# Two layers of attention on one core: the same steps with another table of order, engines and buffers

## The chip, the cores and the metric

The kernel runs on one core of a Trainium2 chip. The metric is the device time of one execution in microseconds. Five engines work beside each other in the core, each through its own queue of instructions in order: TensorE (PE in the profile), VectorE (DVE), ScalarE (ACT), GpSimd (POOL), and SyncE (SP), which here only issues DMA. An engine that waits for a semaphore holds up everything queued behind the waiting instruction.

## The reference

```python
# 1: two-way cross attention of x (8,8,512,64) and state (8,8,32,64), scale 1/8
a     = softmax(scale * x @ state.T);      xread = a @ state
a2    = softmax(scale * state @ x.T);      sread = a2 @ x
y     = concat([xread, sread], axis=2)     # -> (8, 544, 512): 512 x tokens, 32 state tokens
# 2: mixture of 4 attention experts, 2 of them per token, causal
topk, w = two largest of y @ w_gate, softmax over the two
for e in range(4):
    q, k, v = y @ wq[e], y @ wk[e], y @ wv[e]                 # 512 -> 64
    ye  = softmax(causal(scale * q @ k.T)) @ v @ wo[e]        # 64 -> 512
    out += w_e * ye                                           # for tokens that chose e
```

## The kernel before

The eight batches run through the same stages, and several batches are in work at a time. Nearly all matrix products are three products of fp16 halves: a value is kept as a high part and a low part (the rest), and high x high, high x low and low x high are added in a PSUM bank (`PROD`). So nearly every tensor passes through a pair of steps that make the high part (mostly a copy on ACT) and the low part (a subtraction on DVE or POOL).

Per batch, `front` loads and splits x (`xn` to `xh`), turns it by a DMA transpose or by TensorE (`xT`), forms the softmax over the state tokens (scores in a bank, maximum `mb`, exponentials `eb`, sum and reciprocal `sbm`, product `eb` x `sbm`, turned and split into `at`), multiplies the state with the weights (`gs`), and from `at` and `gs` makes values (`v`), keys (`kt`), gate logits (`lg`, weights `wgt`) and queries: a query tile is read out of its bank times a 0/1 mask of the token's experts (`qf` <- bank, `m`; the mask is `m6` in the code), split into `qh` and turned by DMA into `qm`. `probs` computes a query tile's scores for the chosen experts (bank <- `kt`, `qm`), adds the causal mask, takes the maximum (`mx`), the exponential, splits it (`ph`) and has it turned by DMA (`pt`). `reads` multiplies `pt` with `v`, normalises (`su`, `c`, `z`), splits (`zh`, or `zhp` for two tiles at once) and turns; `result` multiplies with `wo` and stores (`o`). The state tokens of two batches are handled together by `side` and `tail`: in `tail`, L1078 makes flags of which experts each of 128 rows has chosen (`m4`, 128 x 4, from `twg`), and the matmul behind it spreads them over a bank (bank <- `identh`, `m`). The trace leaves numbers out of names, so `m4`, `m6` and the maxima of the scores are all `m` there.

None of this sets the order. The calls only record steps: `st.step` keeps an instruction or a group of them with what it reads and writes, 1867 in all. A step that more than one engine could do is recorded with several ways by `small`, `tiny`, `pair`, `split`, `low`, `out_of_bank` and `st.either` (L209): ACT, DVE or POOL for a high part, POOL or DVE for a low part, ACT or DVE for the copy of a bank, and so on. A recorded step has the buffer it belongs to, and a buffer kind has several slots.

`run` (L255) then unpacks three compressed tables from the constant `ORDER`: the order in which the 1867 steps are issued, the way that each takes, and the slot that each buffer gets. It issues every step in that order on line 265, so nearly all instructions of the trace are of L265; they are told apart by the names of their tiles. What stands in the tables was worked out beforehand, and so was `FILL` (L19): a list with one entry for each dummy matmul (`band` 128 x 128 with 128 x 512 zeros into a bank "warm", read by nobody, L511 to L514), whose place in the queue is again in the table. The program holds no other scheduler: each engine runs its instructions in the order issued, and semaphores keep the dependencies.

Of the kernel before, what the change touches and what calls it, by code (L numbers as in the profile page):

```python
# [18 lines left out]
CFG = dict(FILL=(1.0, 1.4, 1.8, 2.2, 2.6, 3.0, 3.4, 3.8, 4.2, 4.6, 5.0,), RA=-1, RG=1, RV=2, RK=2, ZL=3, GP=1, PT=4, ZM=4, SM=4, QM=4, SIDE=32, FB=1, PX=1, PA=2, LB=1, xn=4, W0=-33, PACE=37.0, MU=2, XP=(1,), QP=(0,), LAG=2,  # L19
           FRONT=1.5, FSPAN=1.0, TSPAN=1.3, TOFF=1.2, KT=3, p32=3, ph=2, at=1, et=1, gs=1, xh=4, a2=1, o=4, sn=1, qf=2,  # L20
           n_eb=1, n_e2=1, n_a2t=1, n_xt_tail=2, n_z32=3, n_z=2, n_zh=2, n_tq=1, n_tv=2, n_tpt=1, n_tz=1, n_pt=3, D1=6, DA=6)
ORDER = (
    (
        "c-jrsgJKYB7y!`E|CZKJE!P@qORFurZM9|Fwr$(CZQHhO+xETZB~AhGf-H~^d>}CdKyHW+QIHkFAR%OiypRYALk0+ef{+!90RRF4gMdORh=A"
        "0P4c9;#NC2xK1`K>*E%-wcaF7E0AT1<^valLb!U`w@)u9CB#AQ$eGQkPRjiC^M<scbEVo4|uh4B<5g_>{@Vxa;Q!J?Q8D?%-(1o`na1VUvv1"
        "KFVpTmWx44+o$&cz`FwgQ}1ROTk%a0CnIT)P-u07cW9XD2Dam5~PDhPzYK>F31A~ur$<%Ah-+#aXG}n73cta;VNu_?AR6Z;WcOronR{z!f<Q"
# [2 lines left out]
        "y`-^_17^TNh)<Pp7R-ckkbq`GeH;&oX%WQYF}M$L=uN9}F)V>K_y&Ba6gI$z;7d#45j=*qcn=;xWvqdB;0e5ir|=d0s0u!Vcklw<LrqLb&*3"
        "<HgjM_!>R>}`jHU4de1}?C6<<Lk{03#P2_~X-SR2b?HEfEX;0IL4pU@gV!$<0X>+w6iqh{C^JK+ZGh(D+ecE#rSo_;}RY=K7Yur9uaZs@2b_"  # L30
        "QLkq7kgtr^q~IO2kYSg9Eja<5N^c5cnG@S5Zr`AaTrd(;rIn6ViKB(sc5qFz~3+hKhRX1gst!o%)+EJ8z-Z~WYiO<VM-c<f5D&T;B-t)9+-k"
        "gU>cf>GcY;*15ZqfpC}#zj>NPy598x!8jFbO=nIWQ!UUL&I?;ISOpNm}J$0c`_?1FwGztb#SK5p}DGOzwWSE_@QW%BPVR%gexCOW2H_Ac&sJ"
        "I>9&{o`mdoUpelHpEFgu5|022nTKg-753?!{nwOF1b8W~LRq52MHn4`K#9guf_+QsPPMPJieyW~BYtgN|S(B0h@0sSfp|V;G3YLHL)BBXAL7"
        "Ud@TI82zJQ6h48)sVwKAx^x;#Pz06Z@_Y)XNH3~KA*ft|qbVcCQhiE=MX4g6LE}uAk9yNqPK~$l9D3sp&PCh!EEb^k97&E#QVfOSPR>i`@g;"
        "8H{8W${P;T1Jn|KX3q&T{Sx3Lth<#KcfUtxbL4zKYpUdGb&2G{Wwyo#II7k6<bPJ`F5GMA?^RE5h@1$v8NcpWR!1*}AVIDqb9Wok_~(1SN}W"
        "*kV(XbV@NLR6LdQckEwwWtZb!|L=NYfvL<OO2^8dGbYUPE9E>_oFscliE=Ws>-z~BgEsC`~iL0n|*K)wIn|tOw~9o4j~_o&qHY#CE!*xoOW}"
        "2>O&(a2`A(k(t-ByNJ`3wI1zuubhwvi%0fBF`}hDK=C9b1YVdx(kJb4I*JOVlO%E`Iyy9;-ib~pS8bf0#8Q;WlG)o@hc=F<-oKimFJep6hIh"
        "D+zB)CXE;|h9&spUH!;|VlR=2CuMEGucY{J;e?krvSs+DMBjjU?y!a-0`Z0bWH*X%fBVpSYTe!W$0YW%Q0WQwq+&n`kXn)ihj?Q*wIzg~7aq"
# [1178 lines left out]
```

## Time and profile before

| | before |
|---|---|
| median of 3 runs | 281.39 us (281.38 to 282.41) |
| the profiled execution | 282.26 us, of which the span of the trace is 280.5 us |
| PE matmul busy | 268.0 us, 96% of the span, granted clock 1.00 |
| DVE busy | 251.3 us, 90% |
| ACT busy | 229.0 us, 82% |
| POOL busy | 169.6 us, 60% |
| chain that ended last | PE 69%, DVE 17%, ACT 6%, DMA 4%, issue 2%, SP 1% |

The table is to be read with care, since it averages over stages. The chain of waits is on PE for 69% of the span, though PE is busy for 96%: for a good part of the time PE, DVE and ACT are all busy, and the chain runs over whichever of them is late. A DVE instruction's duration is the time on record, and successive ones overlap a little.

### The profile page before, as it was taken

The numbers are of one execution on the slowest core, as the hardware profiler recorded it, in microseconds if no ns is written. First come the engines' busy times: TensorE is split into PE (matmuls) and PEld (weight loads), VectorE is DVE, ScalarE is ACT, GpSimd is POOL, SyncE is SP. The second block draws the span as 40 slices with busy tenths as digits, with TensorE's granted clock in tenths as the row PEclk, the third lists the DMA queues.
The fourth block names the chain that finished last, engine by engine and source line by source line (L and its number), as shares of the span: only waits on it lengthen the run. The fifth ranks groups of instructions, "written<-read, shape, count | busy, mean of one in ns | idle before, by whom it ended". The sixth has DMA issues, their size and how long they took to land.

```text
span 280.5 us, 9087 instructions
## 1 busy us (share of the span) xinstructions
PE 268.0 (96%) x3408; PEld 179.8 (64%) x3408; DVE 251.3 (90%) x749; ACT 229.0 (82%) x629; POOL 169.6 (60%) x234
## 2 busy tenths in 40 slices
PE   6979899899999899999999999999999999999995
PEld 3856666666486564767677566677576855576763
DVE  3599999999999999999999999899889999889852
ACT  3799898999899789899968988987886779877533
POOL 6534667177886787758757976595473587414210
PEclk9999999999999999999999999999999999999999
DMA  6957899999998969999999999995797979999995
GB/s 184 252 110 178 183 173 206 213 199 166 153 245 170 200 153 222 208 225 227 217 148 192 224 212 193 149 209 139 151 152 159 219 138 173 211 185 191 181 260 208
DMA packets 161804, 53.16 MB, mean 190 GB/s; under 512 B 140640, under 2 KB 157280, under 8 KB 161760
## 3 DMA queue, kind: packets, MB, share of 16 engines
q1 hardware_dynamic: 161760, 52.59, 96.7%
q8 instruction: 26, 0.43, 0.7%
q14 instruction: 18, 0.15, 0.2%
HBM read 11.02 MB, written 8.91 MB: 71 GB/s over the span
## 4 chain that ended last, share of the span: by engine, by line
PE 69%; DVE 17%; ACT 6%; DMA 4%; issue 2%; SPq 1%; DVEq 0%
PE bank L265 69%; DMA pt<-ph 2%; DVE gs L265 2%; DVE p L265 2%; DMA xn<-in_x_dram 2%; ACT e L265 1%; DVE xh L265 1%; DVE m L265 1%; DVE sbm L265 1%; DVE z L265 1%; DVE qf L265 1%; ACT qh L265 1%; SPq L265 1%; DVE xt_tail L265 1%; DVE eb L265 1%
## 5 line engine op out<-in xcount | busy, mean ns | idle before, releaser
L265 ACT ACTIVATE p<-p,mx 128x128 f32<-128x128 f32 (+3 forms) x80 | 41.7, 556 | 6.1 <-DVE su L265 2.4
L265 PE MATMUL bank<-gs,at 128*128 128x260 f16 (+3 forms) x320 | 44.0, 284 | 1.3 <-issue 0.8
L265 PE MATMUL bank<-v,pt 128*128 128x194 f16 (+1 forms) x600 | 42.2, 226 | 0.3 <-DMA pt<-ph 0.3
L265 PE MATMUL bank<-kt,qm 64*128 64x128 f16 (+7 forms) x384 | 42.2, 299 | 0.1
L265 PEld LDWEIGHTS <-pt 128*128 128x128 f16 x600 | 38.5, 98 | 4.0 <-issue 0.9
L265 POOL TENSOR_TENSOR ph<-p,ph 128x768 f16<-128x768 f32 (+1 forms) x18 | 34.7, 1925 | 4.7 <-ACT ph L265 2.3
L265 DVE CUSTOM_DVE_ANT_0 p<-bank,band 128x384 f32<-128x384 f32 (+3 forms) x80 | 36.2, 482 | 1.3 <-PE bank L265 1.0
L265 PEld LDWEIGHTS <-at 128*128 128x128 f16 x288 | 27.3, 97 | 7.9 <-issue 2.1
L265 PEld LDWEIGHTS <-qm 64*128 64x128 f16 (+1 forms) x384 | 21.0, 96 | 17.3 <-issue 8.7
L265 PE MATMUL bank<-at,gs 128*128 128x512 f16 (+1 forms) x116 | 30.0, 396 | 0.1
L265 PE MATMUL bank<-wo_n,z 128*128 128x512 f16 (+1 forms) x114 | 26.1, 368 | 0.0
L265 PE MATMUL bank<-wo_n,zp 128*128 128x512 f16 x84 | 20.4, 379 | 0.4 <-DVE xt_tail L265 0.4
L265 POOL TENSOR_TENSOR qh<-qf,qh 128x768 f16<-128x768 f32 x11 | 18.0, 1644 | 4.3 <-ACT qh L265 2.4
L265 ACT ACTIVATE o<-bank 128x512 f32<-128x512 f32 (+1 forms) x27 | 15.4, 578 | 6.4 <-DMA out_dram<-o 3.3
L265 DVE SCALAR_TENSOR_TENSOR xh<-xn,xh 128x512 f16<-128x512 f32 x26 | 18.6, 718 | 0.5 <-ACT xh L265 0.4
L265 ACT ACTIVATE ph<-p 128x1024 f16<-128x1024 f32 (+1 forms) x17 | 16.5, 970 | 1.9 <-DMA pt<-ph 1.8
L265 PEld LDWEIGHTS <-gs 128*128 128x128 f16 x108 | 9.9, 98 | 12.4 <-issue 2.4
L265 PEld LDWEIGHTS <-z 128*128 128x128 f16 x114 | 10.7, 98 | 10.9 <-issue 0.6
L265 ACT ACTIVATE z<-bank,c 128x64 f32<-128x64 f32 x72 | 16.0, 320 | 0.9 <-POOL c L265 0.8
L265 PEld LDWEIGHTS <-xh 128*128 128x128 f16 x416 | 14.0, 98 | 3.4 <-POOL xh L265 1.5
L265 ACT ACTIVATE xh<-xn 128x512 f16<-128x512 f32 x25 | 15.0, 621 | 1.1 <-DMA xn<-in_x_dram 0.7
L265 ACT ACTIVATE gs<-bank 128x260 f16<-128x260 f32 (+2 forms) x32 | 15.2, 500 | 0.5 <-PE bank L265 0.4
(241 smaller groups left out, 655.5 us busy)
## 6 DMA issues: line engine op xcount, KB each, us to landing
out_dram<-o SPq DMA_DIRECT2D x33, 256.0 KB, 3.0
xn<-in_x_dram SPq DMA_DIRECT2D x14, 512.0 KB, 4.6
xn<-in_x_dram SPq DMA_DIRECT2D x4, 256.0 KB, 3.8
sn<-in_state_dram SPq DMA_DIRECT2D x8, 64.0 KB, 3.9
p<-in_moe_wo_dram SPq DMA_DIRECT2D x2, 256.0 KB, 4.6
pt<-ph SPq DMA_TRANSPOSE x28, 4.8
p<-in_moe_wv_dram SPq DMA_DIRECT2D x1, 384.0 KB, 6.0
p<-in_moe_wk_dram SPq DMA_DIRECT2D x1, 384.0 KB, 4.7
```

What stands on the lines that cost most here:

```text
L265: f(**{k: v.ap() if isinstance(v, View) else v for k, v in kw.items()})
```

## The change

All steps stay what they are, with the same sizes and the same arithmetic. The three tables in `ORDER` are replaced, and `FILL` gets two more entries, so that there are 13 dummy matmuls instead of 11.

```diff
-CFG = dict(FILL=(1.0, 1.4, 1.8, 2.2, 2.6, 3.0, 3.4, 3.8, 4.2, 4.6, 5.0,), ...
+CFG = dict(FILL=(1.0, 1.4, 1.8, 2.2, 2.6, 3.0, 3.4, 3.8, 4.2, 4.6, 5.0, 5.4, 5.8,), ...
 ORDER = (
     (
-        "c-jrsgJKYB7y!`E|CZKJE!P@qORFurZM9|Fwr$(CZQHhO+xETZB~AhGf-H~^d>}CdKyHW+QIHkFAR%OiypRYALk0+ef{+!90RRF4gMdORh=A"
...
+        "c-jTQ17HwP6ac{IpSHHRw6!gJwS~1-jn%Sk+qP}nwr$(CZTrp}ia;UA4Kd&ag&_%KfQ(QaJRmcKLo&z-i6IK|AOHdZgMflBWQ9DC3(`UaWQQ"
...
```

In the unpacked tables 207 of the 1867 steps go to another engine. DVE has 673 steps instead of 663, ACT 503 instead of 521, POOL 228 instead of 220, PE 291 instead of 289 (the two dummies), and SP 174 as before. Most steps on PE keep their place or move by one to five places; on the other engines moves of up to some ten places are common, and a few steps move further. One move on PE is named here because the rows are many: the scores of batch 3's query tile 2 (bank <- `kt`, `qm`, 128 x 384) come five places later when the two dummies are left out of the count, behind two products for keys, two for values and a read of batch 2's probabilities that they stood ahead of. The read of the probabilities made of them comes two places earlier in that count, with the read of tile 1 and a result of batch 2 gone behind it.

The first place to look at is the head of PE's queue. Here `ident` turns a quarter of the first batch's x (`xn`) and the state (`sn`), `band` is a dummy matmul, and `et`, `xT` are the first scores. Before:

```order
L265 MATMUL bank_83<-ident,xn_89 128x128 x4
L265 MATMUL bank_84<-ident,xn_89 128x128 x4
L265 LDWEIGHTS band
L265 MATMUL bank_83<-band 128x512
L265 MATMUL bank_81<-ident,sn_0_86 128x128 x2
L265 MATMUL bank_80<-ident,xn_90 128x128 x4
L265 LDWEIGHTS band
L265 MATMUL bank_83<-band 128x512
L265 MATMUL bank_82<-ident,xn_90 128x128 x4
L265 MATMUL bank_78<-et_91,xT_97 128x2x32 x8
```

And in the changed kernel:

```order
L266 MATMUL bank_82<-ident,xn_89 128x128 x4
L266 MATMUL bank_83<-ident,xn_90 128x128 x4
L266 LDWEIGHTS band
L266 MATMUL bank_82<-band 128x512
L266 MATMUL bank_80<-ident,xn_89 128x128 x4
L266 LDWEIGHTS band
L266 MATMUL bank_82<-band 128x512
L266 MATMUL bank_81<-ident,sn_0_86 128x128 x2
L266 MATMUL bank_84<-ident,xn_90 128x128 x4
L266 LDWEIGHTS band
L266 MATMUL bank_80<-band 128x512
L266 MATMUL bank_83<-et_91,xT_97 128x2x32 x8
```

The loads are issued in the new order of the quarters too. A dummy matmul now stands between the last turned quarter and the first scores, where none stood.

The second place is DVE around the flags of the first `tail`, L1078 (the row 128x4 from `twg`). `qf` is a masked query tile, `et` a transposed block of batch 3's `eb`, `z` a sum of two halves of a result of batch 1, `gs` a low part. Before:

```order
L265 TENSOR_TENSOR qf_142<-bank_77,m_0_138 128x384
L265 SCALAR_TENSOR_TENSOR xt_tail_153<-bank_84,xt_tail_153 64x4x32
L265 TENSOR_TENSOR qf_143<-bank_79,m_0_138 128x384
L265 TENSOR_TENSOR qf_143<-bank_83,m_0_138 128x384
L265 SCALAR_TENSOR_TENSOR twg_189<-wgt_124,own_101,twg_189 128x2
L265 STREAM_TRANSPOSE et_91<-eb_115 128x512
L265 TENSOR_SCALAR m_0_192<-twg_189 128x4
L265 SCALAR_TENSOR_TENSOR gs_121<-bank_82,gs_121 128x512
```

In the changed kernel:

```order
L266 TENSOR_TENSOR qf_143<-bank_78,m_1_139 128x384
L266 SCALAR_TENSOR_TENSOR v_0_108<-bank_84,v_0_108 128x4x64
L266 TENSOR_TENSOR qf_142<-bank_83,m_1_139 128x384
L266 TENSOR_TENSOR qf_142<-bank_82,m_1_139 128x384
L266 SCALAR_TENSOR_TENSOR twg_190<-wgt_124,own_101,twg_190 128x2
L266 TENSOR_TENSOR z_1_167<-z_1_167 128x128
L266 TENSOR_SCALAR m_1_193<-twg_190 128x4
L266 STREAM_TRANSPOSE et_91<-eb_115 128x512
L266 SCALAR_TENSOR_TENSOR gs_121<-bank_80,gs_121 128x512
```

The transpose went behind the flags, a sum that POOL had done later (at 103.10 us of the trace) came in ahead of them, and one low part `xt_tail` went up the queue, as did the other one that stood a few places behind the flags.

The third place is POOL at the same time. `eb` x `sbm` is batch 3's, `qh` the low part of a pair of masked query tiles, `zh` one of batch 1. Before:

```order
L265 TENSOR_SCALAR m_0_138<-wgt_124 128x4x3
L265 TENSOR_TENSOR eb_115<-eb_115,sbm_118 128x1024
L265 AFFINE_SELECT mtail_98<-mtail_98 32x2x32
L265 TENSOR_TENSOR zh_183<-z_1_167,zh_183 128x256
L265 TENSOR_TENSOR qh_141<-qf_142,qh_141 128x2x384
```

In the changed kernel:

```order
L266 TENSOR_SCALAR m_1_139<-wgt_124 128x4x3
L266 TENSOR_TENSOR eb_115<-eb_115,sbm_119 128x1024
L266 TENSOR_TENSOR qh_141<-qf_143,qh_141 128x2x384
L266 TENSOR_TENSOR zh_184<-z_2_168,zh_184 128x256
L266 AFFINE_SELECT both_100<-both_100 32x32
```

The low part `qh` follows `eb` at once, and `zh` comes behind it.

## Rows read from the trace of the kernel before

**Rows 1.** Stretches: length, busy PE, PEld, DVE, ACT, POOL (instructions), clock, DMA, GB/s

```profile
17.03:104.76 87.73, 83.47 (x1188) 57.62 (x1189) 84.86 (x234) 81.03 (x228) 57.46 (x75) 1.00 0.96 180
104.76:250.00 145.24, 144.45 (x1794) 95.60 (x1793) 135.98 (x425) 120.58 (x337) 96.54 (x116) 1.00 1.00 186
```

**Rows 2.** Waits of PE from 17.03 to 104.76: total us, times, longest

```profile
PE bank L265 <- DVE m L265: 1.2, 1, 1.2
PE bank L265 <- DVE eb L265: 1.2, 1, 1.2
PE bank L265 <- DVE qf L265: 0.6, 2, 0.4
```

**Rows 3.** Timeline of DVE at 94 us: start, us, instruction, idle before

```profile
94.45 0.21 DVE L265 SCALAR_TENSOR_TENSOR twg<-wgt,own,twg 128x2 f32<-128x2 f32 x1
94.58 0.70 DVE L265 STREAM_TRANSPOSE et<-eb 128x512 f32<-128x512 f32 x1
95.21 1.61 DVE L265 TENSOR_SCALAR m<-twg 128x4 f16<-128x4 f32 x1
```

**Rows 4.** Timeline of PE at 97 us

```profile
96.88 0.30 PE L265 MATMUL bank<-identh,m 128*64 128x128 f16 x4 [1.20 <-DVE m L265]
```

**Rows 5.** The instructions that write the flags from twg: ns min/median/max

```profile
L265 DVE TENSOR_SCALAR m<-twg x4: 153/288/1615, 95.2 to 248.1; 128x4 f16<-128x4 f32 x4
```

**Rows 6.** Timeline of POOL from 92 us

```profile
92.20 1.91 POOL L265 TENSOR_TENSOR eb<-eb,sbm 128x1024 f32<-128x1024 f32 x1
...
95.16 1.63 POOL L265 TENSOR_TENSOR qh<-qf,qh 128x768 f16<-128x768 f32 x1
```

**Rows 7.** Timeline of ACT at 94 us

```profile
93.80 0.87 ACT L265 ACTIVATE qh<-qf 128x768 f16<-128x768 f32 x1
```

**Rows 8.** Groups of DVE instructions by form: busy us, mean ns, idle before

```profile
L265 DVE SCALAR_TENSOR_TENSOR xh<-xn,xh 128x512 f16<-128x512 f32 x26 | 18.6, 718 | 0.5 <-ACT xh L265 0.4
L265 DVE TENSOR_SCALAR o<-bank 128x512 f32<-128x512 f32 x8 | 5.5, 683 | 0.3 <-PE bank L265 0.3
L265 DVE TENSOR_TENSOR z<-z 128x128 f32<-128x128 f32 x9 | 3.0, 332 | 0.1
L265 DVE SCALAR_TENSOR_TENSOR wn<-p,wn 128x256 f16<-128x256 f32 x5 | 2.1, 415 | 0.0
L265 DVE TENSOR_TENSOR eb<-eb,sbm 128x512 f32<-128x512 f32 x3 | 2.1, 687 | 0.0
L265 DVE TENSOR_SCALAR lg<-bank 128x4 f32<-128x4 f32 x12 | 1.8, 154 | 0.6 <-PE bank L265 0.4
```

**Rows 9.** A product of that size on POOL, by form

```profile
L265 POOL TENSOR_TENSOR eb<-eb,sbm 128x512 f32<-128x512 f32 x1 | 1.0, 1049 | 0.1
```

**Rows 10.** Timeline of PE in the head

```profile
7.55 0.38 PE L265 MATMUL bank<-band 128*128 128x512 bf16 x1
7.94 0.66 PE L265 MATMUL bank<-ident,xn 128*128 128x128 f32 x4
...
15.06 0.81 PE L265 MATMUL bank<-band 128*128 128x512 bf16 x3
```

**Rows 11.** Timeline of PE: scores of batch 3's tile 2, what follows, their read

```profile
133.53 1.73 PE L265 MATMUL bank<-kt,qm 128*128 128x384 f16 x12
135.19 2.76 PE L265 MATMUL bank<-at,gs 128*128 128x512 f16 x12
137.79 0.83 PE L265 MATMUL bank<-gs,at 128*128 128x260 f16 x6
138.46 2.17 PE L265 MATMUL bank<-v,pt 128*128 128x194 f16 x24
140.47 1.49 PE L265 MATMUL bank<-gs,at 128*128 128x260 f16 x12
...
160.26 1.92 PE L265 MATMUL bank<-v,pt 128*128 128x194 f16 x21
```

**Rows 12.** Timeline of SP: the transpose of those probabilities is issued

```profile
150.97 1.47 SPq L265 DMA_TRANSPOSE pt<-ph  x1
```

**Rows 13.** DMA issues of the page: count, median us to landing

```profile
pt<-ph SPq DMA_TRANSPOSE x28, 4.8
```

More of the change, by code (lines that the diff above doesn't have):

```diff
@@ L29 @@
[L29 to L38, printed above, removed]
@@ new lines @@
+        "OO06z$Vbg%|WfI)ijgmvH`Irzg`NDV0=1+0e^5D&`3Do6t*p%8{(Ij9L)AQkvPeyjzjpaPVF+7JiDu>e+tq7VwFAp#?@5}bj8SQ+X-Ca3}hp"
+        "$Jxmx^Nb%!8u3@7oZ-*hXjxi5<zvi2%%U8&O;-p4>jNt6vieHg^i&BT!wIL3s;~lG=!_L5=z50=nnhgIuyliZ~!{NA!rW=VGrDZ9#9PPVh89"
+        "6EuahRg?12zj`Cqg2*zGu)C#)7K3IgkVF$E?&afH!LsJ+4VXy)Ez;;-I-5?qVLSJYGfv_5yLory4Hz5W$LO<9EOYs(rg56L7Z^LrT4})M6#N"
+        "uG6h;L{#w1z1#1oFZzScY3+D3m~@F)$3K!4^0UV_`T5Rl*fG0!G3-m;{qyB_4*7I2BgmbeIo!U^UKw1yBmt;C+}0327mWgErtzm2nXyqSq7*"
+        "aX1SW!+7wZIgpGdfG5p{xzG?xV--w76JZ%Ffks#cA3{=Ei%Vf0E{EjQ7~ervY=Tdr8lHeB@CeppQ+y03p%y-ayYLbc({uO^FW>{bhgYzMYvX"
@@ new lines @@
+        "Hp03YEVe1dxT22xNn{0wFBCsfDg_yfwJ7uCS>_zS+k2K)^*@ekyH4^#)cV_p0TKdBRbrjOJXJ7X98MJ=!$w#S~h8RJn8?22!pC3e90)C>Dyf"
+        "9!~TaRBzi1T+u_;YJ*cn{Wu$#|F3syWvng0>f}Pj=+&P2`A$>NJ+ENho;ID{0skJ8h)aw*b3)hYn+bpF%_kw88{bx2{AP#K)^N_0yA+Qj>3f"
+        "KM`>srexdo82-DLnOiNve&<7XbX!Iw>uH=DZ@GE_zZWKV{QE)6yz=imoa?nH!Bt=h5g{d)!y3=pkiiQ~|H|3?Alm_!qMhd2Ulo)&CTRIBc@C"
+        "RkUo%oJ+pu_Fxg_&p<?#8`%4EA9U%1nFk5XQs(n1w><J>{ZRoE8sY40+=bJd7DJma@_xI*6ySC;g?Pn2mbTG5kl_Nw_y1$9j|rPhdJ^Udx#g"
+        "ID$?hu`+TJ%z|;`i^iw$EY_#|RGyP!11e1gsSj1)Ggy(QNmk4UmDuq*4y9~Zk}C5#EJRV19mA;rm7#cCn6`5^Xh^#_k}lv5K94ytK1b6X^uz"
@@ new lines @@
+        "UBii%Pr+Q89JmUi-P4x`t&kt<MRx`>;&1nuD~*q82N5lX;YcpzQHH+T)J@I5R?*RdkK#dmlEt8z0+kN0saC&&I&iOSPWe2<l>8ehUHG=OsA1"
+        "FTB@C<Rud&0LHIQ47k2)#(Gar5f}RYf>$0O53;z)uHxOn-cP1YDvwhI3?lB*p8}m2Wmxi=^-ZNA(V()Q*s_kt2r6_V=W#=DcFNQ;Rve1!|4&"
+        "$=9F9jMv^CYq`f?fYI0(3L$l-!ccQ}_fTQUa?&r7sp1n9V&lVrv$M5(vj-dm5kjK(E8c!2x0!^YL{E@x6GkwQYe3Tc<Z9K%)^cbg=x%30)N-"
+        "6t-$#5Zk;B>Npd}Th(qg8aA({La@#+3LIC(|7Hg_~)KETZ4&CyQw{Eu$xRf|t?~O3%w_flQ%4xQ2@GNuDPwXe)iiw7iA<Ih>bD7LJ5doQ}6q"
+        "QQl4&cr9h+g%Zl?B_pq+9GsKaQ*O?~r+Fn!m%==iHc&1O;4>V=zMP5kau{!<8S(=EVm_WJ!JL_Q(0mEuX%xr#`5#UvKlYabT#%!91}&08T#R"
@@ new lines @@
+        "301Q+K3Da|E0nyc$sj^wA9jY~1mIga5#o=IhRnPlf!4wUnJiFeWp*+bv(8LpACe1tA@2}W8gS9!Ty;9Ycu_tHLEDXXN4UgHcxv`)(LYPra>="
+        "sM4)pVCBs$$nZd2j~Xh;-fT&e#=chMz^`4?xs4NQ4Z2^`Xd|U1byN=+<=+taeX$ar<r9F)#baqQBKl5{>-)Y6gA{0e3}|_BYwfpc$3uECLCX"
+        "y@=MMnP4%xl<>!2#63Bh7qlc&^H&7>sDWSaLc+!j?P;Pukjr0sP=YR5mTX8eZBA4kkKcd$BkT**k{?2U~v=e{fAN-Yna$UVbkLfCX<6r!nQL"
+        "oV!xlUfvjyrQ>eZ*O%3%BP#+?D_GKTa;O0Fq5my73K4BsH`JlX%Kw_K=#|fm2Fixk=t~fu7?NN+GwXBeRGk5f#!L;v*L+sce<*e4DaMPEp-0"
+        "+r+e%=8^-FOt#BYN+r!Tk36H?vP1SrkesC!%9>a9iRfWTEhVi7@0BBxPxi}BX{kLqja0Tt94xK0jfO~DeNKZpzqHd`GMUfO6mG5Ub+`87-dx"
@@ new lines @@
+        "h7x8Anf2-#qvn!|<IHk%^(ExT>BO_tR5Sq|H5IW4&>tUGLr<#Y!vmle=lE`>W}J1w{Ew_TRUg<Ft2U}3u34qHJzW_zrVp0)y(*A=xpdftv&J"
+        "{Rnc*l`PS`CY80bOl^Nch>e=F*{*rthk-C2s>#5?1DYEK^AF++!d>+Q5Nb>*+47oo?Dm;cTcQ{dun~`nO(M`u7_Q;!4_?oteAUYL#&_mv|e`"
+        "A3R-^~X2soI?QMPSl?}IRcEc*^8yjl(^tHXT>o&qhT44*b`#Rdj*jpQG?<~e*t%Q!UaW>v6>jRB&6KtYQviEk=ZrN?SV-NMNMY?2`+@jn)i+"
+        "1-d#(l7l7V94ACoAE8+h_Y?C0z+CVvqH!m2xTUoBgrxR>*$XUkkN=1}@GySK6VA=N?#mM=pW;X$c*>UzW%{G;toz(><~zPMx`=E}2X0yqvfD"
+        "4~ajYHv"
+    ),
@@ new lines @@
+    (
+        "c-pm;+YZDa2t+;e{~x_s>je<pzHChzS`Y_jq_sah^wo|2-Zn-2`Di9uZuQl(@qNRYlXbpNYSBzU+F%Xj6=O1Vr+m8MH@mb<WtD{@A=J7f+_^"
+        "3xMc2*-awd6xbL%?o0QDGp!C37kgIi01L<!3zZxKWVGI{bYWk^|ids7mvwtq>l;Xp9r-KPGb1wX<fLf?@T-K46GTyLg{w4!0Jgy54iBp8~eo"
+        "T;kNN?}Q%DsN0tU6>6XzJ^~Ri<v9&xKt|I48PI;E`)Q;7W^bv_W4P|qINiNK{7@qvP3|FKB27AV13(-u$^4E6~iPk$N{_KI!;qb4+5|!4=fw"
+        "s2VF)1LI"
+    ),
+    (
+        "c-lo%339|R3=%s3|KkEqTW7|}%9aqI1+-==v??PyF82HVzYsiHUX7lO*+#}F%$30iI<~-6s7N6DJJt6@F|f?R9JlC95Qi5~yq^zXB6Ua*BUR"
+        "iT8-Yq?Tn%vRiUTDTkC1#GRJkhB$%bK+k#rv{w7Ls+lJzlSenmPPZ?Bju;fNvpWGM+)F%E9c2Fwd)uLj>;cFWf!Gt`AZ$*ys^YAvQ1U^OaHW"
+        "i)*1y1%1>#FYR7pqgY}Bx|r^38`wa?1Utu3e<`9bqpe;HDplzOQZTDXQAXT4cX5df;=Z*FY*z}nEh?+XsNkoQMaTFDR!C%ks{z50<x?(L44W"
+        "UzAzUZGq5cM99e<lAcEGE9qHnT*N$*b`cWq$5Pv@t8_z;DY3s@m@vO_1t5^6KUyiKNud%|P?Pa}XG3=6pnkbk`R}+#Tl7O3W;v?Y^qqqE)m^"
+        "S0dB>US#^8EYE?UQKy+bFTm1L|*9k{FevUNyA#la$!250BQD+_`_V2-G%8oDM&Cng%8"
```

45 lines of the change are left out of this document (11 added, 34 removed).

## The prediction

> **What bounds the kernel now.** I read the busy time by stretches first, then what PE waited for in each, and only then the rows around the longest wait. The reader is to see two regimes. From 17.03 to 104.76 us the stretch is 87.73 us long; DVE is busy 84.86 of them (97%), PE 83.47, so PE stands idle for 87.73 - 83.47 = 4.26 us. From 104.76 to 250 us PE is busy 144.45 of 145.24 and idle for 0.79, while DVE has 145.24 - 135.98 = 9.26 us of slack [rows 1]. Ahead of 17 us lie the loads and the first softmax, behind 250 us the last results. So a change of order and engines can take time out of the first regime alone, at most its 4.26 us, and in the second it can only lose.
>
> PE's waits in the first regime name DVE nearly throughout: 1.2 us once for `m`, 1.2 once for `eb` at the regime's very start, and 0.6 in two for `qf` [rows 2].
>
> The wait for `m` is a strange one. PE starts the spreading of the first flags at 96.88 after 1.20 us without work [rows 4]; the flags are 128x4 numbers, yet DVE took 1.61 us over them, 95.21 to 96.82 [rows 3], while the quickest of the four such instructions took 0.153 [rows 5]. Beside it POOL ran the low part `qh`, from 95.16 to 96.79 [rows 6]. DVE ended with POOL to within 0.03 us: I read this as DVE being shut out of SBUF until POOL had finished, at a price of 1.61 - 0.15 = 1.46 us. The Trainium skill ("SBUF — State Buffer", section "Who interferes with whom") states a rule for it: the two engines share a pair of ports, and whichever instruction takes it first keeps it to its end, against a DVE copy or tensor_scalar in a two-port mode or one with two inputs in SBUF. By the rule POOL's instruction, 0.05 us ahead, had the ports; the trace agrees here.
>
> **The change, part by part.** *Engines.* Up to the flags, DVE loses the following after 17 us: the second half of batch 0's `eb` x `sbm` (to POOL), one `o` copy (to ACT), six instructions of about 256 elements or as short (two `wn` and one `zhp` low part to POOL, a `v`, a `gs` and a `wo_n` high part to ACT) and ten small ones (`lg`, `mx`, `su` and the like). By their rows [rows 8]: 0.687 + 0.683 + 6 x 0.415 + 10 x 0.154 = 5.40 us. An instruction of DVE starts about 0.08 us before its forerunner's end (94.45 + 0.21 against 94.58 in [rows 3]), so 18 of them leave 5.40 - 18 x 0.08 = 3.96 us. DVE gains a 512-wide copy into `at` (as the `o` row, 0.683), an `xh` low part that POOL had made in two steps (0.718), two 256-wide high parts (0.83), two sums of `z` (0.66) and ten small ones (1.54): 4.43 - 16 x 0.08 = 3.15. The net is -0.81 us. Two more `xh` high parts and the copy of the state move to DVE ahead of 17 us, where it waits for x anyway; I cost them at nothing, and if they were late the first `mb` would be, by up to half a us.
>
> *Order.* Ahead of the flags the transpose `et` goes behind (-0.70 + 0.08 = -0.62) and one `xt_tail` comes in front (at most a 256-wide instruction, 0.34; half that for a 64-row 128-wide one, +0.2). So DVE reaches the flags 0.81 + 0.62 - 0.2 = 1.2 us sooner, near 94.0 instead of 95.21. PE needs them 1.20 us before 96.88, at 95.68. What matters is who holds POOL then. `qh` cannot start before ACT has its high part, 93.80 + 0.87 = 94.67 [rows 7], and the product ahead of it ends at 92.20 + 1.91 = 94.11 [rows 6]. Flags that come at 94.0 wait 0.1 for the product and are done by 94.3, in the gap before `qh`. Then the whole 1.20 us goes. The bounds are -1.20 (gap met) and 0 (shut out again as long; below nothing if the sum `z` that now stands ahead of the flags is shut out as well, with `qh` starting later: +0.3). I take -1.20: 94.0 is 0.6 us ahead of `qh`'s start, so half of DVE's lead can fail before the gap is missed.
>
> *The other waits of the first regime.* `qf` holds PE for 0.6 us before the flags, and smaller waits make up the rest of the 4.26 us. DVE's lead grows from nothing to 0.81 over that time, and a wait shortened early makes PE come sooner to the next. Between 0 and -0.81 I take half, -0.4. What is late next there is ACT: it is 81.03 us busy in the regime (92%), and it gives up about as much as it gets.
>
> *The head.* The loads come in another order, but the last quarter of x is still the fifth transfer and the dummy matmul behind it now stands between the last turned quarter (started at 7.94) and the scores. Three dummies take 0.81 us and one 0.38 with its tail, so one costs (0.81 - 0.38) / 2 = 0.215; the dummy of 7.55 held the queue until 7.94, 0.39 [rows 10]. It is uncovered, since PE has no gap there and the scores start the first softmax: +0.2 to +0.4, and I take +0.25, near the plain spacing of dummies. The other extra dummy stands in the 1.2 us in which PE waits for `eb` and is hidden. A product on POOL takes 1.049 instead of 0.687 [rows 8, 9], but DVE skips it and gets to `gs` and the next low parts 0.61 us sooner: between -0.61 and 1.05 - 0.69 = +0.36 I take nothing, since PE has other work queued between the two halves.
>
> *After 104.76.* The tables give DVE ten steps more in all, so what left its queue early comes back later: by the same rows some 2.6 us. It has 9.26 us of slack there [rows 1]: nothing. PE's order changes by a few places: nothing. The tail's chain is the same but for copies that change engine: 0, within 0.2 either way.
>
> The sum is -1.20 - 0.4 + 0.25 = -1.35 us. The profiled execution took 282.26, of which 280.5 are the span and 1.76 lie around it; it would take 280.9. The median of the runs is 281.39, 0.87 below the profiled one, and from it follows 281.39 - 1.35 = 280.0 us.
>
> **The rivals.** *The flags are shut out again.* On POOL `qh` now follows `eb` at once, with `zh` moved behind it, so it holds the ports earlier; on DVE a sum of two inputs in SBUF stands ahead of the flags. If they come after 94.67, since DVE's lead did not reach them, they end with `qh`, at 94.67 + 1.63 = 96.3 instead of 96.82. That is -0.5 for the flags; with -0.1 for the other waits and +0.25 in the head, -0.35: 281.0 us. For it speaks that both engines' queues were moved by like amounts; against it, that ACT's high part, which starts `qh`, has no lead. The Trainium skill's rule on the shared ports ("SBUF — State Buffer", as above) gives this outcome whenever `qh` begins first, and an earlier place of the flags alone does not free them.
>
> *Slower: probabilities that come too late.* Batch 3's scores of query tile 2 ended at 133.53 + 1.73 = 135.26; PE read the probabilities at 160.26, 25.0 us later [rows 11]. Now most of what followed the scores goes ahead of them, 135.19 to 137.79 and 138.46 to about 141.8, 5.9 us, and the read comes sooner by the two steps that went behind it, 2.3 us by their like [rows 11] (tile 1's read has half the 24 matmuls of 138.46 to 140.47, 1.0; the result has six of 512 columns, half of 135.19 to 137.79, 1.3): 25.0 - 5.9 - 2.3 = 16.8 us are left. Before, the transpose was issued 150.97 - 135.26 = 15.7 us after the scores [rows 12] and such a one lands 4.8 us after issue [rows 13]: 20.5 us. If mask, exponential and split keep their distance from the scores, PE waits 20.5 - 16.8 = 3.7 us in a regime where nothing gives it back: 281.39 - 1.35 + 3.7 = 283.7. It decides from 16.8 us on. Against it: the 15.7 us are time in queues, and the steps behind the scores have new places too.
>
> *More than forecast.* All of PE's waits for DVE in the first regime but the one at its start go, 1.2 + 0.6, and with them what it waits for through ACT and in pieces, up to 4.26 - 1.2 = 3.1 us in all [rows 1, 2]. With the head's 0.25 that is -2.85: 278.5 us. For it speaks that DVE is 97% busy, and that the waits are chained; against it, ACT at 92%.
>
> **How the numbers follow.** The forecast has 0.44, the flags shut out again 0.21, late probabilities 0.17, more than forecast 0.18. About 0.5% (1.4 us) is what a measurement of this kernel can tell from no change, so faster means under 279.98 and slower over 282.80. The forecast's centre lies on the first line: half of it, 0.22, and the last rival's 0.18 count as faster, 0.40; the other half and nearly all of the first rival as the same, 0.42; the late probabilities and a remainder as slower, 0.18. The forecast's own range is 279.6 (-1.20 - 0.81 + 0.2) to 280.6 (-1.20 + 0.4). The range that should hold the time 8 times in 10 reaches to the third rival at its centre less 0.5 and to a part of the slower one: 278.0 to 282.9.
>
> **What would show it.** The flags take about 0.15 to 0.3 us and PE's wait for `m` in the first regime is gone (forecast), or they end with POOL's `qh` again (first rival). PE's idle time from the first `eb` to the read at which the regimes meet falls from 4.26 to about 2.7 us. The scores start about 0.25 us later than 8.43. PE's idle time in the second regime stays under 1 us; a wait of PE for `pt` of over 1 us there is the slower case. The prediction is wrong if the second regime loses time to DVE, or if PE's idle time in the first does not fall.

## The result: 1.1% slower, and the profile after

The changed kernel takes 284.75 us (median of 18 runs, 284.08 to 287.76), the kernel before 281.59 beside it (18 runs); the ratio is 1.0114 with a 95% interval of 1.0088 to 1.0139. It is slower by about 3.2 us where 1.4 us less was forecast. The profiled execution took 284.08 us, its span 282.2; that of before, 282.26 and 280.5, lay 0.7 us above its median. The two traces therefore differ by 1.8 us (284.08 - 282.26) only. Three runs of the experiments that showed a lower granted clock, one of `early_before` and two of `early_after`, are left out of their medians.

In the stretches of [rows 1] (length, then busy PE, PEld, DVE, ACT, POOL) the changed kernel has:

```profile
17.03:104.76 87.73, 82.91 (x1191) 57.18 (x1191) 84.94 (x233) 81.86 (x230) 59.05 (x74) 1.00 0.92 176
104.76:250.00 145.24, 143.93 (x1752) 94.03 (x1749) 135.08 (x432) 119.61 (x325) 102.59 (x126) 1.00 1.01 188
```

PE stands idle for 87.73 - 82.91 = 4.82 us in the first (4.26 before) and for 145.24 - 143.93 = 1.31 in the second (0.79 before). The regime that was to gain did not, and the one that could "only lose" lost. These are PE's waits in the first, where [rows 2] stood (total, times, longest):

```profile
PE bank L266 <- issue: 1.5, 1, 1.5
PE bank L266 <- DVE z L266: 1.4, 1, 1.4
PE bank L266 <- ACT kt L266: 1.1, 1, 1.1
PE bank L266 <- DVE eb L266: 0.7, 1, 0.7
PE bank L266 <- DVE xt_tail L266: 0.7, 1, 0.7
```

The wait for `m` is gone. The longest wait, at 31.03, has no releaser that the profile shows; the kernel before has one of 0.8 us at 31.10. The flags, where [rows 5] stood, and POOL beside them, where [rows 6] stood:

```profile
L266 DVE TENSOR_SCALAR m<-twg x4: 164/170/172, 96.3 to 249.3; 128x4 f16<-128x4 f32 x4
```

```profile
94.08 1.91 POOL L266 TENSOR_TENSOR eb<-eb,sbm 128x1024 f32<-128x1024 f32 x1
96.56 1.64 POOL L266 TENSOR_TENSOR qh<-qf,qh 128x768 f16<-128x768 f32 x1 [0.57 <-ACT qh L266]
```

All four take 0.17 us. The first starts at 96.34, in the gap between the product's end (95.99) and `qh` (96.56), as forecast, though 2.3 us later than the 94.0 forecast. But a wait for `z` of 1.4 us has come in, and it is new. One goes back from it: to `z` on DVE, and to what DVE did ahead of it. This is DVE's timeline (start, us, instruction, idle before), then POOL's, then PE's:

```profile
88.98 2.08 DVE L266 SCALAR_TENSOR_TENSOR gt<-gt,gt 128x20 f32<-128x20 f32 x1 [0.26 <-ACT gt L266]
91.10 0.18 DVE L266 TENSOR_REDUCE gs<-gt 128x5 f32<-128x20 f32 x1
91.30 0.29 DVE L266 SCALAR_TENSOR_TENSOR xt_tail<-bank,xt_tail 64x128 f16<-64x128 f32 x1
91.61 0.56 DVE L266 TENSOR_TENSOR z<-bank,c 128x384 f32<-128x384 f32 x1
```

```profile
88.90 2.13 POOL L266 TENSOR_TENSOR ph<-p,ph 128x1024 f16<-128x1024 f32 x1
```

```profile
92.22 2.13 PE L266 MATMUL bank<-gs,at 128*128 128x256 f16 x18 [1.44 <-DVE z L266]
```

An instruction of the gate, 128x20 numbers, takes 2.08 us. POOL had begun a 128x1024 low part 0.08 us ahead of it and ended at 91.03; the gate product ended at 91.06. It is the picture of [rows 3] and [rows 6] at another instruction. It occurs a second time, 56 us later, again as DVE, POOL, PE:

```profile
144.96 1.95 DVE L266 SCALAR_TENSOR_TENSOR gt<-gt,gt 128x20 f32<-128x20 f32 x1
```

```profile
144.96 1.92 POOL L266 TENSOR_TENSOR eb<-eb,sbm 128x1024 f32<-128x1024 f32 x1
```

```profile
148.24 0.82 PE L266 MATMUL bank<-gs,at 128*128 128x256 f16 x6 [0.58 <-DVE mx L266]
```

Now the same two pairs in the trace of the kernel before, which the prediction had not looked at (DVE's rows, then POOL's):

```profile
89.09 0.18 DVE L265 SCALAR_TENSOR_TENSOR gt<-gt,gt 128x20 f32<-128x20 f32 x1
...
145.07 0.11 DVE L265 SCALAR_TENSOR_TENSOR gt<-gt,gt 128x20 f32<-128x20 f32 x1
```

```profile
89.13 2.13 POOL L265 TENSOR_TENSOR ph<-p,ph 128x1024 f16<-128x1024 f32 x1
...
145.24 1.91 POOL L265 TENSOR_TENSOR eb<-eb,sbm 128x1024 f32<-128x1024 f32 x1
```

There the gate product was 0.04 us ahead of POOL in the first pair and 0.17 in the second. The change brought POOL forward by 0.23 and 0.28 us and DVE by only 0.11 both times; the order of the two starts turned over in the first pair, the second became a tie that POOL won, and 0.18 us became 2.08 and 0.11 became 1.95. It is no accident of two executions: in the four traces kept with the tables of before at this place POOL begins the `ph` of the first pair 0.04 to 0.15 us behind the gate product, and in the four with the changed tables in which POOL reads there without a guard 0.06 to 0.09 us ahead of it.

Matched matmul by matmul, PE of the changed kernel is 0.16 us ahead of before at batch 2's scores (104.60 instead of 104.76) even so, and 1.5 us behind at the end; the loss of 1.6 us comes in between 148 and 223 us.

### The profile page after: what moved, and what is told of

It is laid out like the page before. It is cut to its first block, busy times and chain, and to the rows that moved or that the text cites. A ratio compares the mean times of both kernels' runs of the same rounds, so it can differ in the third digit from the quotient of the medians.

```text
span 282.2 us, 9119 instructions
## 1 busy us (share of the span) xinstructions
PE 268.9 (95%) x3410; PEld 179.4 (64%) x3410; DVE 252.5 (89%) x759; ACT 229.2 (81%) x624; POOL 176.3 (62%) x243
## 4 chain that ended last, share of the span: by engine, by line
PE 57%; DVE 18%; ACT 12%; issue 4%; POOL 4%; DMA 4%; SPq 1%; DVEq 0%; POOLq 0%; ACTq 0%
PE bank L266 57%; DVE p L266 3%; ACT p L266 2%; DMA tpt<-ptl 2%; DVE gt L266 2%; DMA xn<-in_x_dram 2%; DVE sbm L266 2%; DVE gs L266 1%; DVE xh L266 1%; DVE eb L266 1%; DVE a L266 1%; ACT xh L266 1%; ACT gs L266 1%; POOL ph L266 1%; ACT kt L266 1%
## 5 line engine op out<-in xcount | busy, mean ns | idle before, releaser
L266 ACT ACTIVATE p<-p,mx 128x128 f32<-128x128 f32 (+3 forms) x80 | 40.5, 557 | 4.0 <-POOL mx L266 2.3
L266 PE MATMUL bank<-v,pt 128*128 128x194 f16 (+1 forms) x600 | 41.6, 226 | 0.0
L266 DVE CUSTOM_DVE_ANT_0 p<-bank,band 128x256 f32<-128x256 f32 (+3 forms) x80 | 36.2, 482 | 2.7 <-PE bank L266 2.1
L266 POOL TENSOR_TENSOR ph<-p,ph 128x768 f16<-128x768 f32 (+1 forms) x17 | 33.2, 1952 | 3.9 <-DVE c L266 2.1
L266 POOL TENSOR_TENSOR qh<-qf,qh 128x768 f16<-128x768 f32 x11 | 19.6, 1788 | 4.8 <-ACT qh L266 3.3
L266 ACT ACTIVATE o<-bank 128x512 f32<-128x512 f32 (+1 forms) x28 | 16.4, 587 | 7.4 <-PE bank L266 5.4
L266 POOL TENSOR_TENSOR c<-su,wgt 128x6 f32<-128x6 f32 (+1 forms) x24 | 7.4, 307 | 23.2 <-DVE su L266 22.5
L266 ACT ACTIVATE z<-bank,c 128x64 f32<-128x64 f32 x82 | 18.4, 324 | 4.0 <-POOL c L266 2.7
L266 ACT ACTIVATE v<-bank 128x256 f16<-128x256 f32 x39 | 14.6, 390 | 3.8 <-PE bank L266 3.8
```

The costliest lines, as they stand in the source:

```text
L266: f(**{k: v.ap() if isinstance(v, View) else v for k, v in kw.items()})
```

## The experiments

The theory (ports): two new lockouts of the gate product make the whole loss. (A lockout is short here for a DVE instruction that is stretched to the end of a POOL instruction.) The rivals: one lockout makes the other (rival A below), or what the first loses is given back at the read where the regimes meet (rival B); the DVE work that was moved behind 104.76 us is what costs ("put-back" in the expectations); other waits take the place of those that go ("hops"); the gate product is slow for a reason other than POOL's reads; or the new order or the new engines cost the time as such.

**Which half of the program.** `early_before` has the tables of before up to batch 2's scores and the changed ones behind; `early_after` the other way round. The changed part has 11 dummies in both. The edit is told in words, since the tables are compressed.

```diff
 for n in memoryview(steps).cast("H"):   # the table holds, for early_before:
+    order, ways and slots of before      up to the scores of batch 2 (step 668)
+    order, ways and slots of after       for every step not yet issued
```

> Order, engines and buffers of the kernel before up to the scores of batch 2 at 104.76 us, and those of the changed kernel (with 11 dummy matmuls) for every step that is left. Rival put-back or anything else behind 104.76 us: most of the loss, +1.5 to +3.2 us against before (1.005 to 1.011). Theory ports: the lockout at 145 us may come again or not, +0.3 to +1.5 us. If the loss lies ahead of 104.76 us: within 0.5 us of before.

> Order, engines and buffers of the changed kernel (with 11 dummy matmuls) up to the scores of batch 2, and those of the kernel before for every step that is left. In the two traces TensorE reaches these scores 0.16 us sooner in the changed kernel. Theory put-back: within 0.5 us of before or up to 1 us faster (0.996 to 1.002). Theory ports: the lockout of the gate at 89 us is in it and that of the flags is not: within 0.6 us of before either way. If the loss lies ahead of 104.76 us: +1.5 to +3 us (1.005 to 1.011).

`early_before`: 284.03 us (11 runs), ratio 1.0087 [1.0049, 1.0124]; the flags are shut out (1.617 us), the first gate product is not, the second is (1.95 us from 146.02, beside a POOL product from 146.01). `early_after`: 284.84 us (4 runs), 1.0121 [1.0071, 1.0171]; the first gate product is shut out (2.10 us), and at the seam PE waits 2.3 us for `e`, which neither parent does. Each half loses by itself, and each with its own lockout; but the seams have waits of their own (0.7 us for `p` in `early_before`), so the halves' sizes are not to be read as shares. By the numbers alone the theory missed twice: it had +0.3 to +1.5 us and within 0.6, and +2.4 and +3.4 came, nearest to what was set down for put-back and for a loss ahead of 104.76. What decides for the lockouts comes next.

**Both lockouts taken away.** Ahead of each of the two POOL instructions (steps 467 and 1205) a tiny POOL instruction reads one column of the gate product (596, 1019). POOL then cannot begin before the product has ended.

```diff
+GUARDS = {467: 596, 1205: 1019}
 for n in memoryview(steps).cast("H"):
     s = self.all[n]
+    if n in GUARDS:   # done: the output of the step named
+        self.nc.gpsimd.tensor_scalar(out=seen[:, 0:1], in0=done[:, 0:1], scalar1=0.0, scalar2=1.0, op0=ALU.add, op1=ALU.mult)
```

> The changed kernel with one tiny GpSimd instruction (it reads one column of the gate's result gt) ahead of two GpSimd products, the low part ph at 88.9 us and the product eb x sbm at 145.0 us, so that GpSimd takes neither up before VectorE has finished the gate's 128x20 instruction. Theory ports: these two VectorE instructions took 2.08 and 1.95 us in the changed kernel because GpSimd held the shared ports; they fall to about 0.2 us, TensorE's waits of 1.44 us (at 92.2) and 0.58 us (at 148.2) behind them go for the most part, and the time falls by 1.3 to 2 us, to 282.8 to 283.5 (1.004 to 1.007 of the kernel before). Rival put-back (VectorE's work that was moved behind 104.76 us is what costs): no more than 0.4 us, 284.4 or above (1.010). Rival hops (other waits take the place of those two at once): the two instructions get short and the time stays within 0.5 us of 284.75.

Measured: 281.28 us (12 runs), ratio to before 1.0001 [0.9974, 1.0028]. DVE, then POOL:

```profile
89.04 0.18 DVE L270 SCALAR_TENSOR_TENSOR gt<-gt,gt 128x20 f32<-128x20 f32 x1 [0.19 <-ACT gt L270]
```

```profile
89.31 0.19 POOL L268 TENSOR_SCALAR seen<-gt 128x1 f32<-128x1 f32 x1 [0.29 <-DVE gt L270]
89.46 2.13 POOL L270 TENSOR_TENSOR ph<-p,ph 128x1024 f16<-128x1024 f32 x1
```

Two instructions of 0.19 us, which do nothing but make POOL wait, are worth 284.75 - 281.28 = 3.47 us by the medians (before had 281.59 and 281.62 beside them), and 1.13 points or 3.2 us by the ratios. POOL's low part begins 0.56 us later, and PE has no new wait of over 0.3 us. That is more than the 1.3 to 2 us expected: PE gains 1.6 us at 92.22 and 0.74 at 148.24, and further on 0.3 at 150.63 and 0.3 at 155.06 that the expectation had not counted. Put-back falls with it, since every step keeps its engine and its place, and so do hops. The loss against before is explained; that the forecast's gain does not appear is not (see the end of the next section).

**One at a time.** The same with one guard each.

```diff
-GUARDS = {467: 596, 1205: 1019}
+GUARDS = {467: 596}     # after_guard_1
+GUARDS = {1205: 1019}   # after_guard_2
```

> The changed kernel with one tiny POOL instruction ahead of the low part ph that ran at 88.90: it reads one column of the second gate product on DVE, so ph cannot begin before that product has ended. The other product (144.96) is left as it was. Theory (two separate lockouts on the shared ports): the product takes about 0.2 us instead of 2.08, PE's wait for z at 92.22 (1.44) goes, the second product still takes about 1.95 us, and the time is 284.75 - 1.6 = 283.15 (ratio to the kernel before 1.0055). Rival A (one cause, the first lockout starting a cascade that makes the second): 281.3, as with both guards. Rival B (only the second counts, what the first loses is given back at the read where the regimes meet): 284.7.

> The changed kernel with the tiny POOL instruction only ahead of the product eb x sbm that ran at 144.96. Theory: the gate product there takes about 0.2 us instead of 1.95, the loss that the changed kernel took from 148 us on (+0.45 at 153.7 to +1.6 at 223.5) goes, the first product still takes about 2.08; 284.75 - 1.6 = 283.15 (ratio 1.0055). Rival A (cascade from the first): no gain, since the first still stands: 284.7. Rival B: 281.3.

Measured: 283.28 us (ratio 1.0081 [1.0049, 1.0112]) and 283.12 us (1.0084 [1.0053, 1.0114]). The gains by medians are 1.47 and 1.63, together 3.10 of the 3.47. In the first the second gate product is still shut out (1.94 us), in the second the first (2.08): neither makes the other, so rival A falls. PE gains 1.60 us at 92.22 in the first, and 0.75 + 0.30 + 0.35 = 1.40 at 148.24, 150.63 and 155.06 in the second: the first guard is worth something by itself, and rival B falls. By the ratios, which compare runs of one round, the sum is less sure: 0.33 + 0.30 of 1.13 points, with intervals of 0.3 each. The traces show that each gives back a part. In the first, of the 1.9 us that PE is ahead of the changed kernel before this row, 1.06 are left from it on:

```profile
116.02 1.52 PE L270 MATMUL bank<-v,tpt 128*64 128x259 f16 x24 [0.97 <-DMA tpt<-ptl]
```

In the second, PE is 0.65 us behind the changed kernel when it comes to 148.24, having waited for two DMA transposes (0.3 us for `tpt`, 0.4 for `a2t`). And a third near miss came out the other way in the first (DVE, then POOL); PE shows no wait of over 0.2 us behind it, so it has no price there:

```profile
117.32 1.33 DVE L270 SCALAR_TENSOR_TENSOR gt<-gt,gt 128x16 f32<-128x16 f32 x1 [0.39 <-ACT gt L270]
```

```profile
116.97 1.65 POOL L270 TENSOR_TENSOR ph<-p,ph 128x768 f16<-128x768 f32 x1
```

Where neither guard or both stand, the same gate product is ahead of its POOL instruction by 0.11 us (118.77 and 118.88 in the changed kernel) and takes 0.13 us.

**The dose.** Nothing is waited for in addition; only POOL's two instructions are cut into halves (the edit is shortened).

```diff
+HALVES = {467: 512, 1205: 16}
-    f(**args)
+    for part in [slice(0, w), slice(w, 2 * w)]: f(out, in0 and in1 cut to part)
```

> The changed kernel with the two POOL instructions (ph at 88.90, eb x sbm at 144.96) issued as two instructions over half the columns each, and nothing waited for in addition. Theory (DVE is shut out until the POOL instruction that has the ports ends): each gate product ends with the first half, so it takes about 1.1 us instead of 2.08 and about 1.0 instead of 1.95; PE's two losses fall by about half to two thirds, 284.75 - 1.6 to 2.2 = 282.6 to 283.2 (ratio 1.0035 to 1.0055). Rival (the duration of the gate products is a slow form of their own, or they wait for a semaphore from POOL): they keep their 2 us and the time stays at 284.7 or above.

Measured: 282.81 us, ratio 1.0059 [1.003, 1.0088]. The two gate products:

```profile
89.58 1.11 DVE L267 SCALAR_TENSOR_TENSOR gt<-gt,gt 128x20 f32<-128x20 f32 x1 [0.24 <-ACT gt L267]
...
145.18 1.08 DVE L267 SCALAR_TENSOR_TENSOR gt<-gt,gt 128x20 f32<-128x20 f32 x1
```

and POOL, where a row holds both halves:

```profile
89.50 2.27 POOL L267 TENSOR_TENSOR ph<-p,ph 128x512 f16<-128x512 f32 x2
...
145.18 2.05 POOL L267 TENSOR_TENSOR eb<-eb,sbm 128x512 f32<-128x512 f32 x2
```

POOL's first halves take 1.16 and 1.05 us. The gate product's duration follows the one POOL instruction that had begun ahead of it, not the work POOL has in all: half as long, 1.1 us each. The rival of a slow form of its own falls.

**What of POOL shuts DVE out.** POOL's two instructions write the same output and read nothing.

```diff
+                if n in (467, 1205):
+                    f = lambda out, **_: self.nc.gpsimd.memset(out, 0.0)
```

> The changed kernel with the same two POOL instructions replaced by a POOL memset of the same output (128x1024), which reads nothing from SBUF. The kernel leaves out the low part of one pair of batch 1's probabilities and batch 5's product eb x sbm. Theory (the lock is on the shared pair of ports, which a POOL instruction that only writes does not take): the two gate products take about 0.2 us each, and the time is near 281. Rival (any POOL instruction in SBUF shuts out the two-input product until it ends): each ends with the memset, so they take as long as what is left of it.

Measured: one execution, 281.63 us. DVE, then POOL:

```profile
88.90 0.18 DVE L265 SCALAR_TENSOR_TENSOR gt<-gt,gt 128x20 f32<-128x20 f32 x1 [0.24 <-ACT gt L265]
...
144.33 0.18 DVE L265 SCALAR_TENSOR_TENSOR gt<-gt,gt 128x20 f32<-128x20 f32 x1
```

```profile
88.79 0.96 POOL L264 MEMSET ph<- 128x1024 f16 x1
...
144.31 0.95 POOL L264 MEMSET eb<- 128x1024 f32 x1
```

POOL again began first, by 0.11 and 0.02 us on record, and the gate products took 0.18 us beside it and ended 0.67 and 0.75 us ahead of the memsets. In the same trace the third near miss, beside a POOL instruction that does read, came out the other way (DVE, then POOL):

```profile
117.01 1.56 DVE L265 SCALAR_TENSOR_TENSOR gt<-gt,gt 128x16 f32<-128x16 f32 x1
```

```profile
116.90 1.64 POOL L265 TENSOR_TENSOR ph<-p,ph 128x768 f16<-128x768 f32 x1
```

A semaphore set by POOL at its end would have held the gate products here too, so that rival falls. It is what POOL reads that shuts out a product with two inputs in SBUF, as far as a memset stands for an instruction that only writes. The Trainium skill ("SBUF — State Buffer", section "Who interferes with whom") states just that: two SBUF inputs contend with a GpSimd instruction that reads SBUF, "not with one that only writes it". The runs agree: 2.08 and 1.95 us beside POOL instructions that read, 0.18 and 0.18 beside those that only write.

**Order and engines apart.** `order_only` has the changed order and slots with the 207 steps put back to the engines of before; `ways_only` the old order and slots with the new engines. The edit is told in words.

```diff
-steps, ways, slots = after, after, after
+steps, ways, slots = after, before, after     # order_only
+steps, ways, slots = before, after, before    # ways_only
```

> The order and slots of the changed kernel with the engines of the kernel before (the 207 steps put back). Theory (the loss came by two near misses of some hundredths of a us, which hang on every small step ahead of them): the two gate products meet other neighbours, the lockouts of small DVE instructions in the trace fall elsewhere, and the time goes by how many of them PE waits for: 281 to 287, with a PE wait behind each. Rival (the new order costs the time by itself): the time stays near 284.7 with both gate products at about 0.2 us. Rival (the new engines cost it): 281.5.

> The order and slots of the kernel before with the engines of the changed kernel. Theory: as in the other, neither half carries the loss by itself; 281 to 287 by the lockouts that PE waits for, and the flags may be shut out again since the order around them is the old one. Rival (the new engines cost the time by themselves): near 284.7 without lockouts of small instructions that PE waits for. Rival (the new order cost it): 281.5.

Measured: 319.02 us (1.1342 [1.1275, 1.1409]) and 306.65 us (1.0908 [1.0835, 1.0981]). Both lie far outside what I had expected, 281 to 287, and the rivals' numbers are as far off. In `order_only` PE waits for many (total, times, longest):

```profile
PE bank L263 <- DVE mx L263: 5.2, 4, 2.1
PE bank L263 <- DVE kt L263: 4.1, 3, 2.2
PE bank L263 <- DVE z L263: 3.9, 4, 1.6
```

Lockouts are many there. DVE products of two inputs, `tensor_scalar` and copies with all inputs in SBUF that were over 0.6 us longer than the quickest of their kind, each beside a POOL instruction that reads, number 18 in `order_only` (22.2 us in all) and 9 in `ways_only` (9.0 us), against 2 in before and 2 in the changed kernel. How much of this PE pays is not shown. A step that moves to another engine also stands in that queue at a place meant for something else and may hold up what is behind it; that is argued, and I have not taken the rest apart. Both gate products are shut out again in `order_only` (2.08 us from 94.00, 1.94 from 156.37) and neither in `ways_only` (0.42 and 0.11 us). That points to the new order as what brought them, but in kernels that differ from the changed one by much else.

**A version that beats both.** The kernel before with one guard: POOL's `qh` waits for the flags of [rows 3]. It was measured twice.

```diff
+GUARDS = {618: 643}   # in the kernel before: qh waits for the first flags
```

> The kernel before with one tiny GpSimd instruction that reads the flags ahead of the low part qh at 95.2 us, so that GpSimd cannot hold the ports while VectorE writes the flags. Theory ports: the flags take 0.16 to 0.3 us instead of 1.61, TensorE's wait of 1.20 us for them falls to 0.3 or less, and the time is 0.8 to 1.3 us less than before (0.995 to 0.997). Rival hops: the flags get short, but TensorE waits for something else by then, and the time is within 0.4 us of before. If the ports were not the cause, the flags stay over 1 us long.

> The kernel before with the tiny POOL instruction ahead of qh that reads the flags, a second time, since its interval touched 1. Theory (the flags' lockout costs PE 1.2 us and nothing takes its place): PE's wait for m is gone and the time is 281.5 - 1.0 = 280.5 (ratio 0.996 to 0.998). Rival (the first result was chance, or what the flags give back is lost at the read where the regimes meet): 281.5 (ratio 1.000).

Measured: 280.56 us, ratio 0.9972 [0.9942, 1.0002], and 280.76 us, 0.9966 [0.9934, 0.9997]. In the second, DVE and then POOL:

```profile
94.60 0.13 DVE L270 TENSOR_SCALAR m<-twg 128x4 f16<-128x4 f32 x1
```

```profile
94.81 0.19 POOL L268 TENSOR_SCALAR seen<-m 128x1 f32<-128x1 f16 x1
94.96 1.64 POOL L270 TENSOR_TENSOR qh<-qf,qh 128x768 f16<-128x768 f32 x1
```

The flags take 0.13 us instead of 1.61, and `qh` begins 0.36 us behind the start of the flags. It gives 0.3%, some 0.9 us of the 1.20 that PE had waited; the first interval touches 1, the second does not. In both traces PE gains 1.3 us at the flags. In the second it gives nearly all of it back at 126.58, in a wait of 1.08 us for `su` that the kernel before does not have; in the first it does not.

## Why the prediction was wrong

**The flags (-1.20): right in what became of the wait, in part by luck.** They met the gap ahead of `qh`, and PE's wait for `m` went. But DVE's lead was mis-sized: without the lockout ahead of them the flags come at 94.70 (in the guarded kernel), 0.5 us sooner than before and not 1.2. That would have missed `qh` at the 94.67 of the forecast. The gap was met by 0.2 us because ACT's high part came later too, at 93.99 + 0.84 = 94.83, so that `qh` began at 94.91. The single guard on the kernel before shows the term by itself: PE gains 1.3 us at the flags and the kernel 0.9.

**The other waits of the first regime (-0.4): the sum fits one trace once the lockout is away, the term is not shown.** In the guarded kernel the regime runs from the first `eb` to batch 2's scores as here:

```profile
16.75 0.63 PE L270 MATMUL bank<-ident,eb 128*128 128x128 f32 x4 [0.69 <-DVE eb L270]
...
102.95 1.75 PE L270 MATMUL bank<-kt,qm 128*128 128x128 f16 x24
```

That is 86.20 us instead of 87.73, 1.53 less where -1.20 - 0.4 = -1.6 were forecast; PE's idle time in it falls to 86.20 - 82.73 = 3.47 us and not to 2.7. But the kernel before with its guard, where the flags alone are freed, has 87.47 and 86.59 us in its two traces, so that one trace cannot size a term of 0.4. What the waits were made of differs: `eb` fell from 1.2 to 0.7 and `qf` went, while a wait for `kt` rose from 0.2 to 1.1 us and the one without a releaser from 0.8 to 1.6. [rows 2] had left that one out, third in its view, and 0.9 us for ACT: of 5.2 us of waits DVE has 3.5, so "nearly throughout" said too much.

**The head (+0.25): its size is open.** In this pair of traces the scores start at 8.33 instead of 8.43, 0.1 us sooner. The dummy shows 0.22 us between its start and that of the scores, as foretold; the last quarter is turned at 7.62 instead of 7.94 [rows 10], as it lands:

```profile
7.62 0.66 PE L266 MATMUL bank<-ident,xn 128*128 128x128 f32 x4 [0.49 <-DMA xn<-in_x_dram]
8.11 0.38 PE L266 MATMUL bank<-band 128*128 128x512 bf16 x1
8.33 0.89 PE L266 MATMUL bank<-et,xT 128*128 128x64 f32 x7
```

The landing differs between executions by more than the term: the scores start between 7.33 and 8.43 in four traces with the head of before, and between 8.00 and 9.14 in six with the changed head. From the start of the last turned matmul to the scores it is 0.11 us in all four and 0.32 to 0.87 in the six, so the price is there, and at least 0.2 us.

**The late probabilities (the slower rival): did not happen.** The distance from the scores to their read did shrink, to 159.41 - 141.17 = 18.2 us (16.8 foretold, 25.0 before), below the 20.5 of [rows 12, 13]:

```profile
139.44 1.73 PE L266 MATMUL bank<-kt,qm 128*128 128x384 f16 x12
...
159.41 2.76 PE L266 MATMUL bank<-v,pt 128*128 128x194 f16 x31
```

Yet PE did not wait. The last transpose of a `pt` ahead of the read was issued at 151.47, 10.3 us after the scores instead of 15.7. The 15.7 were not a fixed distance, as the argument against the rival had it.

**No term for new lockouts, in the first regime's sum and in "After 104.76 ... nothing": the step that failed.** I had read [rows 3] and [rows 6] rightly, as DVE shut out by POOL, and then treated it as the one accident of the trace, to be freed or not. Every other instruction was costed at the mean of its row [rows 8], whatever stood beside it. The same accident can come wherever a small DVE instruction with its inputs in SBUF starts within a tenth of a us of a long POOL instruction that reads, and a new table of order deals those starts anew. The term that was missing was a list of the near misses in the trace of before. The first gate product escaped by 0.04 us, at a price of 1.90 (2.08 - 0.18), and 1.4 to 1.6 of that were PE's; it fell in the very regime that was to gain. The second escaped by 0.17, at 1.84 (1.95 - 0.11), and 1.4 were PE's. The two together are nearly the 3.2 us. The slack of 9.26 us in the second regime [rows 1] did not help: slack that is spread over 145 us does not cover 1.8 us lost at one place, when PE waits for the next thing behind it in DVE's queue. My first rival had the mechanism and put it back on the flags; the slower side had another mechanism.

**What is open.** Without its two lockouts the changed kernel takes 281.28 us, as much as before (1.0001 [0.9974, 1.0028]), and not the 280.0 forecast. The kernel before without its one lockout took 280.56 in the same round, 0.7 us less, though the forecast's terms other than the flags add up to -0.15. So the rest of the new tables gains nothing, and may cost 0.7 us; the two traces, with spans of 279.0 us each, do not show where. The lockout of the flags is no accident of one execution, since `early_before`, with the tables of before at that place, has it too (1.62 us from 95.09). How often each lockout occurs in the executions that were not profiled is not known.

## What to carry to other kernels

When order or engines move, list the near misses first: each short DVE instruction with two inputs in SBUF (or a `tensor_scalar` from there) that starts within some tenths of a us of a long POOL instruction that reads SBUF, on either side of it, and price a turn-over at what POOL then has left. Where PE waits behind such a pair, let POOL's instruction wait for the DVE one by a dependency; here 0.19 us on POOL saved 0.9 to 1.7 us each. Then measure: a pair further on can turn over in its place, as the third near miss did twice here. An order and an assignment of engines that were worked out together are tested together.
